# One fused attention and two-layer expert kernel: scores placed behind q, a shorter preparation of the extra unit, and first loads in another order

## The chip, the cores and the metric

The kernel runs on one core of one Trainium2 chip. The metric is the device time of one execution in microseconds (us); lower is better. The core has TensorE (PE, matrix products), VectorE (DVE), ScalarE (ACT) and GpSimd (POOL) for computing, SyncE (SP) for issuing transfers, and 16 DMA engines. Each engine works through its own list of instructions in order and waits on semaphores for the others. PE writes to PSUM, which has eight banks; a bank is written again only when its readers are done.

## The reference

Three parts, one after another, on 8 batches of 576 tokens with 8 heads of 64 (4608 tokens of width 512):

```python
def sm_attn(qq, kk, vv):                      # softmax(scale * qq kk^T) vv
    ...
p_packed = sm_attn(p, k, v)                   # 32 packed rows per head
x = sm_attn(q, p_packed, p_packed)            # 576 rows per head
# first expert layer: 8 experts, D = 512, F = 1024, one expert per token
y[mask] = gate_w[mask, None] * (np.maximum(x[mask] @ w1[e], 0) @ w2[e])
# second layer: only tokens with x @ w_skip > 0, other weights
out[do_compute] = xc + gate_w * (np.maximum(xc @ w1[e], 0) @ w2[e])
```

## The kernel before

The work runs batch by batch, with everything transposed so that features lie on partitions. Per batch the main generator `gen_M` makes two halves of 288 tokens: `stage1` (lines 728, 733, 734) forms h in eight tiles of six matmuls each, `stage2` (line 749) forms y in four tiles of 24. Each fp32 product is made of three products of a high and a low part: `hh` is ACT's rounded copy of h and `hl` DVE's remainder, `W2h`/`W2l` and `Q1h`/`Q1l` are such pairs of weights. A main batch assumes one expert for the whole batch; tokens that do not fit are handled as extra units (`gen_x`) and, in the second layer, by lists (`gen_pick` and others).

The smaller steps are put between the matmuls of `gen_M` by a planner, `Weave`. It has 48 steps per batch: 8 for h and 16 for y in each half. A side generator gets a window such as `(8, 0.5, 1.06)`: 8 steps spread from 50% to 106% of the loop. With `TE` its steps on PE go to the borders of y tiles. These sides matter here:

- `gen_S(b)` (from line 382), two batches ahead: `heads` (line 385) writes the scores s1 of packed rows p against k into four banks, DVE takes their maxima mx (407) and the negated nm (413), ACT the exponentials a1 (417), PE transposes those (434), and pv, pk, PKT follow.
- `gen_pre(b)` (from 627), one batch ahead: reads the expert index e1 into a register (631), loads W1 by it (642), and multiplies it by PKT (`heads` again, called q1), so that Q1 = W1 folded with the packed values; ACT and DVE cut it into Q1h and Q1l (lines 623, 624).
- `gen_T`, `gen_R(b)` (580): second scores and the products L for the gate of the first layer; `x_flags` (970) turns sums csA into flags of extra units.

SP issues nearly all loads in its list's order. For batch 0 the quarters of k go by SP and ACT in turn. PE fills waits in the head with idle products ("keep", line 347).

Of the kernel before, what the change touches and what calls it, by code (L numbers as in the profile page):

```python
# [11 lines left out]
BF16 = mybir.dt.bfloat16  # L12
# [106 lines left out]
def attn_moe_kernel(ctx, tc, q, k, v, p, wg, w11, w12, w21, w22, out):  # L119
# [18 lines left out]
    def ct(name, shape, dt=F32, fill=None, eng=None):  # L138
        t = const.tile(shape, dt, name=name)
        if fill is not None:  # L140
            (eng or nc.vector).memset(t, fill)
        return t
# [5 lines left out]
    iot = ct("iot", [128, 128])  # L148
    pid = ct("pid", [128, 1])
    E8 = ct("E8", [128, E])  # L150
    M5 = ct("M5", [128, 5, 2, NXP])
    once = ct("once", [128, 5, 32])
    tri = ct("tri", [128, 128])
    ones = ct("ones", [128, 128])
# [214 lines left out]
        return [(t[:, 0:n], a[:, 0:n]), (t[:, n:], a[:, n:])]  # L369

    def load_k(b, *eng):
        ins = load(b, "kT", k, [2, 4, HALF], quarters, eng)
        load(b, "pT", p, [128], lambda t, a: [(t, a)], eng[:1])
        return ins

    def load_v(b, *eng):
        return load(b, "v", v, [10, 4, D], halves, eng)
# [249 lines left out]
    def gen_pre(b):  # L627
        d = us[b]
        while "e1" not in st[b]:
            next(A)  # L630
        e1 = nc.sync.value_load(e1i[0:1, b:b + 1], min_val=0, max_val=E - 1)
        d["e1"] = e1
        W1 = []

        def lw(n):
            for z in range(2):
                if n:
                    w = us[b]["y"].rearrange("p t c -> p (t c)")[:, F * z:F * (z + 1)]
                    w = w.rearrange("p (h f) -> p h f", h=2)
                else:  # L640
                    w = wcp.tile([128, 2, 512], F32, tag="W1c", name="W1c")
                nc.sync.dma_start(
                    out=w,
                    in_=w11[dsn(e1, 1), n, z].rearrange("o p h f -> p (o h) f"),
                )
                W1.append(w)

        lw(0)
        if b > 1:
            us[b]["y"] = bulk.tile([128, 4, S], F32, tag="y", name="y1", bufs=2)  # L650
        lw(1)
        yield
        A2 = st[b]["A2"]
        d["A2h"] = [q1p.tile([128, 2, HALF], F32R, tag=f"A2h{i}", name="A2h") for i in range(2)]
        d["A2l"] = [q1p.tile([128, 2, HALF], F32R, tag=f"A2l{i}", name="A2l") for i in range(2)]

        def halve(hf):
            return split(d["A2h"][hf], d["A2l"][hf], A2[:, :, hf * HALF:(hf + 1) * HALF], nc.vector)

        Q1h = q1p.tile([128, 2, F], F32R, name="Q1h")  # L660
        Q1l = q1p.tile([128, 2, F], F32R, name="Q1l")
        d["Q1"] = (Q1h, Q1l)
        PKT = st[b]["PKT"]
        def product(n):
            ps = [mt("q1") for _ in range(2)]
            heads(ps, PKT, lambda hp: W1[2 * n + hp // 2][:, hp % 2, :], start=True, stop=True)
            return ps

        def cut(n, ps, cuts=()):
            sl = slice(512 * n, 512 * n + 512)  # L670
            for x in range(2):
                with ExitStack() as order:
                    for ins in cuts:
                        order.enter_context(tc.issue_after(ins))
                    split(Q1h[:, x, sl], Q1l[:, x, sl], ps[x], nc.vector)
                yield

        cuts = halve(0)
        if b:
            yield  # L680
            halve(1)
            yield TE
            ps = [product(n) for n in range(2)]
            for n in range(2):
                yield from cut(n, ps[n])
        else:
# [34 lines left out]
    def stage1(lh, ll, rh, rl, kt, hh, hl, hf=None):  # L721
        n_, nr = hh.shape[2], rh.shape[2]
        for f in range(8):
            ps = mt("h")
            n = 0
            for t in range(kt):
                for l, r in ((lh, rh), (lh, rl), (ll, rh)):
                    nc.tensor.matmul(  # L728
                        out=ps[:, 0:nr], lhsT=l[:, t, 128 * f:128 * f + 128], rhs=r[:, t, :],
                        start=(n == 0), stop=(n == 3 * kt - 1),  # L730
                    )
                    n += 1
            nc.scalar.activation(out=hh[:, f, :], in_=ps[:, 0:n_], func=ACTF.Relu)  # L733
            nc.vector.scalar_tensor_tensor(  # L734
                out=hl[:, f, :], in0=ps[:, 0:n_], scalar=0.0, in1=hh[:, f, :].bitcast(F32),
                op0=ALU.max, op1=ALU.subtract,
            )
            if nr > n_:
                nc.vector.tensor_scalar(out=hf[:, f, :], in0=ps[:, n_:nr], scalar1=0.0, scalar2=None, op0=ALU.max)
            yield  # L740
# [196 lines left out]

    us[0]["y"], us[1]["y"] = (bulk.tile([128, 4, S], F32, tag="y", name="y1", bufs=2) for _ in range(2))
    k0 = load_k(0, nc.sync, nc.scalar)
    nc.scalar.dma_start(out=wgAB, in_=wg)  # L940
    behind = mybir.DependencyInfo(mybir.DependencyClass.Sync, mybir.DependencyReason.DATA)
    tc.add_manual_dep(load_v(0, nc.sync)[0], k0[0].name, behind)
    with tc.issue_after(k0[2]):
        load_q(0, nc.sync)
        load_k(1)
        load_q(1)
# [18 lines left out]

    def x_flags():
        f0 = mt("f0")
        for z in range(2):
            for s in range(5):
                nc.tensor.matmul(  # L970
                    out=f0[0:NXP, B * z:B * z + B], lhsT=M5[:, s, z, :], rhs=csA[:, s, :], start=(s == 0), stop=(s == 4)
                )
        FL = X["FL"]
        Fv = FL.rearrange("p (b z) -> p b z", z=2)
# [57 lines left out]
                out=EB["W2"][:, :, 128 * t:128 * t + 128], in_=w12[dsn(ex, 1), t].rearrange("o p f c -> p (o f) c")  # L1032
            )

    def gen_x(X):
        li = X["li"]
        A2g, bd, xt, hr, hx, ro, yx = (X[n] for n in ("A2", "bd", "xt", "hq", "hx", "rq", "y"))
        for hp in range(4):
            r = slice(32 * hp, 32 * hp + 32)
            nc.vector.tensor_tensor(  # L1040
                out=bd[r, :, hp, :], in0=A2g[r], in1=X["gB"][r].unsqueeze(1).to_broadcast([32, 2, UW]), op=ALU.mult
            )
        yield
        ps = mt("xt")
        for x in range(2):
# [119 lines left out]

    def gen_pick(d):

        gc, f, cu, po, Og = d["gc"], EB["f"], EB["cu"], EB["po"], EB["O"]
        nc.vector.tensor_scalar(out=f, in0=gc, scalar1=0.0, scalar2=None, op0=ALU.is_gt)
        for j in range(1, 5):  # L1170
            nc.vector.tensor_tensor(out=cu[:, j:j + 1], in0=cu[:, j - 1:j], in1=f[:, j - 1:j], op=ALU.add)
        yield TE
        ps = mt("pk")
        nc.tensor.matmul(out=ps[:, 0:5], lhsT=trib, rhs=f, start=True, stop=False)
        nc.tensor.matmul(out=ps[:, 0:5], lhsT=oneb, rhs=cu[:, 0:5], start=False, stop=True)
        nc.vector.tensor_copy(po, ps[:, 0:5])
        for j in range(5):
            nc.vector.tensor_scalar(
                out=Og[:, j, :], in0=iot, scalar1=po[:, j:j + 1], scalar2=gc[:, j:j + 1],
                op0=ALU.is_equal, op1=ALU.mult,  # L1180
            )
# [178 lines left out]
    for b in range(B):  # L1360
# [4 lines left out]
        if b + 2 <= B:  # L1365
# [8 lines left out]
                sides.append((gate(b, 2), 2, 0.4, 0.48))  # L1374
            if b + 2 < B:
                if b:
                    plan = ((NS, 0.06, 0.18, TE), (NT, 0.18, 0.477), (8, 0.5, 1.06))
                else:
                    plan = ((2, 0.04, 0.075), (5, 0.115, 0.235), (NT, 0.235, 0.48), (8, 0.5, 1.06))
            else:  # L1380
                plan = ((NS, 0.06, 0.17, TE), (NT, 0.17, 0.33), (NR, 0.34, 0.52))
            sides += [(part(A, n), n, *w) for n, *w in plan]
        if b + 1 < B:
            pre = gen_pre(b + 1)
            w2 = gen_w2(w12, us[b + 1], False)
            sides.append((chain(part(pre, 1), part(w2, 1)), 2, 0.5, 0.6))
            sides.append((part(pre, 2), 2, 0.7, 0.85))
            sides.append((pre, 5, 0.88, 1.0, TE))
            if b + 2 == B:
                sides.append((gen_gB(b + 1), 2, 0.97, 1.0))  # L1390
            sides.append((w2, 4, 0.76, 1.1))
        if b < B - 1:
            W = Weave(gen_M(b), NM, sides, EVERY if b else 2)
        if b == B - 2:
            W.run(0.53)
            run_gen(A)
            a_ctx.close()
            ep = e1_ctx.enter_context(tc.tile_pool(name="ep", bufs=1))
# [13 lines left out]
            X["bd"] = X["ro"][:, 256:512].rearrange("p (x h c) -> p x h c", x=2, c=UW)  # L1412
            X["li"] = xs.tile([1, 3], I32, name="xli")
            cx = X["cx"] = xs.tile([32, 3], F32, name="cx")
            EB["cu"] = xs.tile([128, 5], BF16, name="ecu")
            nc.vector.memset(EB["cu"], 0.0)
            nc.vector.memset(X["bd"], 0.0)
            EB["gc"] = [xs.tile([128, 5], F32, name=f"egc{i}") for i in range(2)]
            EB["gB"] = [xs.tile([128, S], F32, name=f"egB{i}") for i in range(2)]
# [26 lines left out]
        elif b == B - 1:  # L1446
# [22 lines left out]
            with c.Else():  # L1469
                first_half(True)  # L1470
            d0.update(e_load(lyA, iA, 0, True, False))
            W = Weave(gen_M(b, (1,)), NM // 2, [])
            W.run(1 / 3)
            q1_ctx.close()
# [31 lines left out]
    EB["hr"] = X["h"]  # L1506
    EB["xT"] = X["ro"].rearrange("p (t c) -> p t c", t=4)
    ds = {}
    cA = nc.values_load(lyA[3:4, 0:1], min_val=0, max_val=1)

    def gen_load(s):
        d = e_load(lyB, slice(s + 1, s + 2), s + 1, True)
# [201 lines left out]
```

## Time and profile before

| | |
|---|---|
| time, median of 3 runs | 596.32 us (596.19 to 596.82) |
| the profiled execution | 596.14 us, of which span 594.4 us |
| PE busy | 578.4 us (97%) |
| DVE, ACT, POOL busy | 337.4, 216.7, 135.3 us |
| mean granted clock of PE | 0.998 |

The span is the time from the first to the last instruction that the profiler saw. Busy time of PE is counted from the start of a matmul to its modelled end, so matmuls that overlap are not counted twice, and a busy PE can still be off its usual pace. In the timeline a row is a run of like instructions: its start, the time it covers, and in brackets how long the engine was idle before it and for whom it waited. The trace counts one fp32 matmul as two records in some shapes, so block s of 16 matmuls is 32 records.

### The profile page before, as it was taken

The numbers are of one execution on the slowest core, as the hardware profiler recorded it, in microseconds if no ns is written. First come the engines' busy times: TensorE is split into PE (matmuls) and PEld (weight loads), VectorE is DVE, ScalarE is ACT, GpSimd is POOL, SyncE is SP. The second block draws the span as 40 slices with busy tenths as digits, with TensorE's granted clock in tenths as the row PEclk, the third lists the DMA queues.
The fourth block names the chain that finished last, engine by engine and source line by source line (L and its number), as shares of the span: only waits on it lengthen the run. The fifth ranks groups of instructions, "written<-read, shape, count | busy, mean of one in ns | idle before, by whom it ended". The sixth has DMA issues, their size and how long they took to land.

```text
span 594.4 us, 14695 instructions
## 1 busy us (share of the span) xinstructions
PE 578.4 (97%) x5901; PEld 532.2 (90%) x5902; DVE 337.4 (57%) x1001; ACT 216.7 (36%) x475; POOL 135.3 (23%) x122
## 2 busy tenths in 40 slices
PE   7799999999999999999999999999999999999996
PEld 5479899989989989989989898899999999999795
DVE  3878468558638738747746864446846336163110
ACT  3463452542553362344345234224414325052110
POOL 4051331241060150141133105020301220140032
PEclk9999999999999999999999999999999999999999
DMA  8987869567647737826715526996147592722064
GB/s 332 354 320 277 343 243 343 173 242 277 246 171 255 281 148 283 305 74 256 271 41 199 206 71 195 323 320 217 48 132 275 72 374 79 204 53 114 1 99 63
DMA packets 35994, 123.05 MB, mean 207 GB/s; under 512 B 5696, under 2 KB 15680, under 8 KB 29888
## 3 DMA queue, kind: packets, MB, share of 16 engines
q1 hardware_dynamic: 30352, 115.80, 53.2%
q0 software_dynamic: 3968, 4.85, 6.2%
q10 hardware_dynamic: 1584, 1.25, 0.7%
q8 instruction: 50, 0.82, 0.6%
q14 instruction: 40, 0.33, 0.2%
HBM read 92.62 MB, written 29.26 MB: 205 GB/s over the span
## 4 chain that ended last, share of the span: by engine, by line
PE 74%; another core or an unknown queue 6%; DVE 5%; DMA 5%; issue 3%; SPq 2%; ACT 1%; POOL 1%; POOLq 0%; DVEq 0%
PE y L749 30%; PE h L728 23%; PE y L1338 9%; PE s L385 3%; PE q L385 2%; DMA out_dram<-iXR 2%; SPq L1031 1%; DMA gm2d<-gT 1%; PE L L793 1%; PE pv L447 1%; PE at L434 1%; DMA pT<-in_p_dram 1%; DMA egB<-gm2d 1%; PE L L580 1%
## 5 line engine op out<-in xcount | busy, mean ns | idle before, releaser
L749 PE MATMUL y<-hh,W2h 128*128 128x288 f32 x512 | 155.4, 303 | 0.5 <-ACT hh L733 0.5
L749 PE MATMUL y<-hl,W2h 128*128 128x288 f32 x512 | 151.3, 296 | 0.8 <-DVE hl L734 0.6
L749 PE MATMUL y<-hh,W2l 128*128 128x288 f32 x512 | 150.8, 294 | 0.0
L749 PEld LDWEIGHTS y<-hh,W2h 128*128 128x128 f32 x512 | 96.0, 187 | 10.7 <-issue 6.6
L749 PEld LDWEIGHTS y<-hl,W2h 128*128 128x128 f32 x512 | 96.2, 188 | 1.4 <-DVE hl L734 1.4
L624 POOL TENSOR_TENSOR W2l<-W2c,W2h 128x1024 fp32r<-128x1024 f32 x28 | 67.0, 2400 | 131.1 <-ACT W2h L623 112.0
L749 PEld LDWEIGHTS y<-hh,W2l 128*128 128x128 f32 x512 | 96.4, 188 | 0.3 <-issue 0.3
L728 PE MATMUL h<-A2h,Q1h 128*128 128x288 f32 x256 | 77.3, 302 | 2.0 <-DVE T L527 2.0
L734 DVE SCALAR_TENSOR_TENSOR hl<-h,hh 128x288 fp32r<-128x288 f32 x128 | 57.2, 452 | 35.1 <-ACT hh L733 34.1
L728 PE MATMUL h<-A2h,Q1l 128*128 128x288 f32 x256 | 75.5, 296 | 0.0
L728 PE MATMUL h<-A2l,Q1h 128*128 128x288 f32 x256 | 75.3, 295 | 0.0
L733 ACT ACTIVATE hh<-h 128x288 fp32r<-128x288 f32 x128 | 52.3, 413 | 61.3 <-PE h L728 57.0
L728 PE MATMUL h<-eXh,eW1h 128*128 128x288 f32 x192 | 57.7, 300 | 0.7 <-DMA x2d<-y 0.7
L1338 PE MATMUL y<-ihh,iW2h 128*128 128x288 f32 x192 | 56.8, 296 | 0.0
L1338 PE MATMUL y<-ihh,iW2l 128*128 128x288 f32 x192 | 56.6, 295 | 0.0
L728 PE MATMUL h<-eXl,eW1h 128*128 128x288 f32 x192 | 56.5, 295 | 0.0
L1338 PE MATMUL y<-ihl,iW2h 128*128 128x288 f32 x192 | 56.5, 294 | 0.0
L728 PE MATMUL h<-eXh,eW1l 128*128 128x288 f32 x192 | 56.5, 294 | 0.0
L728 PEld LDWEIGHTS h<-A2h,Q1h 128*128 128x128 f32 x256 | 48.0, 187 | 6.1 <-ACT Q1h L623 2.9
L728 PEld LDWEIGHTS h<-A2h,Q1l 128*128 128x128 f32 x256 | 48.1, 188 | 0.6 <-DVE Q1l L624 0.5
L623 ACT CAST W2h<-W2c 128x1024 fp32r<-128x1024 f32 x30 | 31.7, 1055 | 45.4 <-DMA W2c<-in_w_dram 18.3
L728 PEld LDWEIGHTS h<-A2l,Q1h 128*128 128x128 f32 x256 | 48.1, 188 | 0.0
(300 smaller groups left out, 949.8 us busy)
## 6 DMA issues: line engine op xcount, KB each, us to landing
eW<-in_w_dram SPq DMA_DIRECT2D x8, 2048.0 KB
W2c<-in_w_dram SPq DMA_DIRECT2D x30, 512.0 KB
y<-in_w_dram SPq DMA_DIRECT2D x18, 512.0 KB
v<-in_v_dram SPq DMA_DIRECT2D x7, 1280.0 KB
W1c<-in_w_dram SPq DMA_DIRECT2D x16, 512.0 KB
kT<-in_k_dram SPq DMA_DIRECT2D x7, 1152.0 KB
qT<-in_q_dram SPq DMA_DIRECT2D x7, 1152.0 KB
x2d<-y SPq DMA_DIRECT2D x7, 1152.0 KB
```

Source lines behind the costliest of these rows:

```text
L385: m = nc.tensor.matmul(out=out[x][32 * hp:32 * hp + 32], lhsT=lhsT[64 * x:64 * x + 64, 32 * hp:32 * hp + 32], rhs=rhs(hp)[64 * x:64 * x + ...
L434: last = nc.tensor.transpose(ats[x][:, 128 * j:128 * j + 128], a1[:, x, 128 * j:128 * j + 128], ident).ins
L447: nc.tensor.matmul(out=pv[x][32 * hp:32 * hp + 32], lhsT=aT[:, 4 * x + j, 32 * hp:32 * hp + 32], rhs=vm[:, 2 * hp + x, j, :], start=(j == ...
L580: nc.tensor.matmul(out=L[32 * i:32 * i + 32, 0:LN], lhsT=gs[:, g, :], rhs=A2[:, g, c:c + LN], start=(g == 0), stop=(g == 1),)
L623: a = nc.scalar.copy(out=hi, in_=x)
L624: z = eng.tensor_tensor(out=lo, in0=x, in1=hi.bitcast(F32), op=ALU.subtract)
L728: nc.tensor.matmul(out=ps[:, 0:nr], lhsT=l[:, t, 128 * f:128 * f + 128], rhs=r[:, t, :], start=(n == 0), stop=(n == 3 * kt - 1),)
L733: nc.scalar.activation(out=hh[:, f, :], in_=ps[:, 0:n_], func=ACTF.Relu)
L734: nc.vector.scalar_tensor_tensor(out=hl[:, f, :], in0=ps[:, 0:n_], scalar=0.0, in1=hh[:, f, :].bitcast(F32), op0=ALU.max, op1=ALU.subtract,)
L749: nc.tensor.matmul(out=ps[:, 0:HALF], lhsT=l[:, f, :], rhs=r[:, f, :], start=(n == 0), stop=(n == 23))
L793: nc.tensor.matmul(out=L[32 * i:32 * i + 32, 0:LN], lhsT=wgB[:, t, :], rhs=y1[:, t, LC[i]:LC[i] + LN], start=(t == 0), stop=(t == 3),)
L1338: nc.tensor.matmul(out=ps[:, 0:HALF], lhsT=l[:, f, 128 * t:128 * t + 128], rhs=r[:, f, c], start=(n == 0), stop=(n == 23))
```

## The change

```diff
-    M5 = ct("M5", [128, 5, 2, NXP])
+    M5 = ct("M5", [128, 5, 2, NXP], BF16)
+    csb = ct("csb", [128, 5, B], BF16)
...
     def load_k(b, *eng):
-        ins = load(b, "kT", k, [2, 4, HALF], quarters, eng)
-        load(b, "pT", p, [128], lambda t, a: [(t, a)], eng[:1])
-        return ins
+        load(b, "pT", p, [128], lambda t, a: [(t, a)], eng[1:])
+        return load(b, "kT", k, [2, 4, HALF], quarters, eng)
...
+        ea = e1 if b else nc.scalar.value_load(e1i[0:1, b:b + 1], min_val=0, max_val=E - 1)
...
-                nc.sync.dma_start(
-                    out=w,
-                    in_=w11[dsn(e1, 1), n, z].rearrange("o p h f -> p (o h) f"),
-                )
+                eng, e = (nc.scalar, ea) if b == 0 and z > n else (nc.sync, e1)
+                eng.dma_start(out=w, in_=w11[dsn(e, 1), n, z].rearrange("o p h f -> p (o h) f"))
...
     k0 = load_k(0, nc.sync, nc.scalar)
-    nc.scalar.dma_start(out=wgAB, in_=wg)
...
-    tc.add_manual_dep(load_v(0, nc.sync)[0], k0[0].name, behind)
-    with tc.issue_after(k0[2]):
+    v0 = load_v(0, nc.sync)
+    tc.add_manual_dep(v0[0], k0[0].name, behind)
+    with tc.issue_after(v0[1]):
+        wg0 = nc.sync.dma_start(out=wgAB, in_=wg).ins
+    with tc.issue_after(wg0):
         load_q(0, nc.sync)
         load_k(1)
         load_q(1)
...
     def x_flags():
         f0 = mt("f0")
+        nc.vector.tensor_scalar(out=csb, in0=csA, scalar1=0.0, scalar2=None, op0=ALU.is_gt)
...
-    ... lhsT=M5[:, s, z, :], rhs=csA[:, s, :], ...
+    ... lhsT=M5[:, s, z, :], rhs=csb[:, s, :], ...
...
-    def gen_x(X):
+    def gen_x(X, tail=None):
+        last = tail["hl"] if tail else None
...
+            with tc.issue_after(last) if last is not None else nullcontext():
                 nc.vector.tensor_tensor(
                     out=bd[r, :, hp, :], in0=A2g[r], in1=X["gB"][r].unsqueeze(1).to_broadcast([32, 2, UW]), op=ALU.mult
                 )
...
-        for j in range(1, 5):
-            nc.vector.tensor_tensor(out=cu[:, j:j + 1], in0=cu[:, j - 1:j], in1=f[:, j - 1:j], op=ALU.add)
...
-        nc.tensor.matmul(out=ps[:, 0:5], lhsT=oneb, rhs=cu[:, 0:5], start=False, stop=True)
+        for j in range(4):
+            nc.tensor.matmul(
+                out=ps[:, j + 1:5], lhsT=oneb, rhs=f[:, j:j + 1].to_broadcast([128, 4 - j]), start=False, stop=(j == 3)
+            )
...
-                    plan = ((NS, 0.06, 0.18, TE), (NT, 0.18, 0.477), (8, 0.5, 1.06))
+                    plan = ((NS, 0.06, 0.18, TE), (NT, 0.18, 0.477), (1, 0.5, 0.57), (7, 0.815, 1.06, TE))
...
-                plan = ((NS, 0.06, 0.17, TE), (NT, 0.17, 0.33), (NR, 0.34, 0.52))
+                plan = ((NS, 0.06, 0.17, TE), (NT, 0.17, 0.33), (4, 0.34, 0.41), (NR, 0.45, 0.56))
...
-            sides.append((pre, 5, 0.88, 1.0, TE))
+            sides.append((pre, 5, 0.8, 1.0, TE))
...
-            W.run(0.53)
+            W.run(0.565)
```

`us[0]["hl"]` is set by `stage1` to its last hl instruction. In the same way batch 0 has its plan's last entry replaced, and `cA`, a register loaded for a branch, is loaded in the source before the last half batch instead of behind it.

The instruction lists show where it moves. On PE in batch 1, at the end of s and of q before (h is L728, y is L749, both scores and q come from line 385):

```order
679 L728 MATMUL h<-A2h,Q1l 128x288
680 L385 MATMUL s_1741<-kT,pT 32x288
...
695 L385 MATMUL s_1752<-kT,pT 32x288
696 L749 MATMUL y<-hh,W2h 128x288
...
767 L749 MATMUL y<-hh,W2l 128x288
768 L385 MATMUL q_1887<-W1c,PKT 32x512
...
783 L385 MATMUL q_1898<-y_1663,PKT 32x512
784 L749 MATMUL y<-hh,W2h 128x288
```

and the same place in the changed kernel:

```order
727 L749 MATMUL y<-hh,W2l 128x288
728 L385 MATMUL q_1822<-W1c,PKT 32x512
...
743 L385 MATMUL q_1833<-y_1673,PKT 32x512
744 L385 MATMUL s_1844<-kT,pT 32x288
...
759 L385 MATMUL s_1855<-kT,pT 32x288
760 L749 MATMUL y<-hh,W2h 128x288
```

Before, 72 y lie between s and q and 24 behind q; after, 48 y lie ahead of q, s follows at once, and 48 y lie behind it.

On PE in batch 6, where L (L580) is formed for batch 7, before:

```order
2402 L749 MATMUL y<-hh,W2l 128x288
2403 L580 MATMUL L<-A_5126,gs 32x160 x2
2404 L749 MATMUL y<-hh,W2h 128x288
2405 L749 MATMUL y<-hl,W2h 128x288
2406 L580 MATMUL L<-A_5126,gs 32x160 x4
2407 L749 MATMUL y<-hh,W2l 128x288
2408 L580 MATMUL L<-A_5126,gs 32x160 x2
2409 L749 MATMUL y<-hh,W2h 128x288
```

and after:

```order
2413 L749 MATMUL y<-hl,W2h 128x288
2414 L749 MATMUL y<-hh,W2l 128x288
2415 L580 MATMUL L<-A_5136,gs 32x160 x8
2416 L749 MATMUL y<-hh,W2h 128x288
2417 L749 MATMUL y<-hl,W2h 128x288
```

The three pieces are one, 12 y further on.

SP's first transfers, before:

```order
3 L358 DMA kT<-in_k_dram 128x576 x2
4 L358 DMA pT<-in_p_dram 128x128
5 L358 DMA v<-in_v_dram 128x1280 x2
6 L358 DMA qT<-in_q_dram 128x1152 x2
7 L358 DMA kT<-in_k_dram 128x2304
8 L358 DMA pT<-in_p_dram 128x128
9 L358 DMA qT<-in_q_dram 128x2304
```

and after:

```order
3 L359 DMA kT<-in_k_dram 128x576 x2
4 L359 DMA v<-in_v_dram 128x1280 x2
5 L944 DMA wgAB<-in_wg_dram 128x256
6 L359 DMA qT<-in_q_dram 128x1152 x2
7 L359 DMA pT<-in_p_dram 128x128
8 L359 DMA kT<-in_k_dram 128x2304
9 L359 DMA qT<-in_q_dram 128x2304
```

The first p has gone to the front of ACT's list, ahead of ACT's two quarters of k, and wgAB has come from ACT's list to behind v; p of batch 1 stands ahead of its k.

## Rows read from the trace of the kernel before

**Rows 1.** The page's chain that ended last: share of the span by engine.

```profile
PE 74%; another core or an unknown queue 6%; DVE 5%; DMA 5%; issue 3%; SPq 2%; ACT 1%; POOL 1%; POOLq 0%; DVEq 0%
```

**Rows 2.** By stretch: length; busy PE, PEld, DVE, ACT, POOL; clock, DMA share, GB/s.

```profile
110.00:157.00 47.00, 47.00 (x551) 43.89 (x543) 30.79 (x96) 19.24 (x46) 12.18 (x6) 1.00 0.67 242
```

**Rows 3.** Timeline, PE around block s: start, length, engine, line, operation, count.

```profile
156.48 0.29 PE L728 MATMUL h<-A2h,Q1l 128*128 128x288 f32 x1
...
158.07 0.30 PE L749 MATMUL y<-hl,W2h 128*128 128x288 f32 x1
```

**Rows 4.** Timeline, PE, a block with its own shape behind it.

```profile
185.05 1.20 PE L385 MATMUL s<-qT,PKT 64*32 64x288 f32 x32
186.04 0.25 PE L385 MATMUL s<-wgAB,PKT 64*32 64x32 f32 x13
```

**Rows 5.** Timeline around q of batch 6, with ACT and DVE.

```profile
361.98 1.09 PE L385 MATMUL q<-W1c,PKT 64*32 64x512 f32 x16
362.00 1.05 ACT L623 CAST W2h<-W2c 128x1024 fp32r<-128x1024 f32 x1 [2.95 <-PE y L749]
...
362.86 1.06 PE L385 MATMUL q<-y,PKT 64*32 64x512 f32 x16
...
363.16 2.06 ACT L623 CAST Q1h<-q 128x512 fp32r<-128x512 f32 x4
363.78 1.89 DVE L624 TENSOR_TENSOR Q1l<-q,Q1h 128x512 fp32r<-128x512 f32 x3 [1.23 <-ACT Q1h L623]
```

**Rows 6.** Timeline, DVE and ACT behind block s.

```profile
158.49 1.54 DVE L407 TENSOR_REDUCE mx<-s 128x1 f32<-128x288 f32 x4
...
160.25 0.50 ACT L417 ACTIVATE a<-s,nm 128x288 f32<-128x288 f32 x1 [2.47 <-DVE nm L413]
```

**Rows 7.** Timeline, PE in batch 6: first and last y around L's pieces.

```profile
337.27 0.29 PE L749 MATMUL y<-hh,W2l 128*128 128x288 f32 x1
...
340.05 0.30 PE L749 MATMUL y<-hl,W2h 128*128 128x288 f32 x1
```

**Rows 8.** Timeline, PE, L as one block in an earlier batch.

```profile
179.30 0.73 PE L580 MATMUL L<-A,gs 128*32 128x160 f32 x16
179.95 0.40 PE L728 MATMUL h<-A2h,Q1h 128*128 128x288 f32 x1
```

**Rows 9.** Timeline, PE, the flags.

```profile
344.30 1.41 PE L970 MATMUL f<-csA,M 128*72 128x8 f32 x20
345.56 0.38 PE L728 MATMUL h<-A2h,Q1h 128*128 128x288 f32 x1
```

**Rows 10.** Timeline, PE, two bf16 matmuls of the selection.

```profile
529.52 0.18 PE L1174 MATMUL pk<-if,trib 128*128 128x5 bf16 x1
...
529.56 0.17 PE L1175 MATMUL pk<-ecu,oneb 128*128 128x5 bf16 x1
```

**Rows 11.** Timeline, DVE and PE in batch 7: bd, and y.

```profile
369.14 3.14 DVE L1040 TENSOR_TENSOR xro<-xA,xgB 32x64 f32<-32x64 f32 x4 [0.59 <-DVE y L767]
...
378.21 0.40 PE L749 MATMUL y<-hl,W2h 128*128 128x288 f32 x1 [0.63 <-DVE hl L734]
```

**Rows 12.** Chain of waits in the head: start, length, what.

```profile
1.94 5.16 DMA pT<-in_p_dram
...
7.24 1.21 PE s L385 x32
...
17.60 1.38 issue
```

**Rows 13.** Table by stretch, the head (columns as in rows 2).

```profile
4.00:6.00 2.00, 2.00 (x8) 1.41 (x6) 0.00 (x0) 0.00 (x0) 0.65 (x1) 1.00 1.05 398
19.00:20.00 1.00, 1.00 (x25) 0.44 (x24) 0.59 (x2) 0.00 (x0) 0.00 (x0) 1.00 0.18 61
26.80:36.07 9.27, 8.62 (x67) 6.90 (x68) 8.48 (x21) 8.82 (x22) 2.56 (x3) 1.00 0.76 312
```

**Rows 14.** DMA issues of the head: one line of the list.

```profile
wgAB<-in_wg_dram ACTq DMA_DIRECT2D x1, 128.0 KB
```

More of the change, by code (lines that the diff above doesn't have):

```diff
@@ L733, in stage1 @@
             nc.scalar.activation(out=hh[:, f, :], in_=ps[:, 0:n_], func=ACTF.Relu)
-            nc.vector.scalar_tensor_tensor(
+            ins = nc.vector.scalar_tensor_tensor(
                 out=hl[:, f, :], in0=ps[:, 0:n_], scalar=0.0, in1=hh[:, f, :].bitcast(F32),
@@ L737, in stage1 @@
             )
+            us[0]["hl"] = ins.ins
             if nr > n_:
@@ L970, in x_flags @@
                 nc.tensor.matmul(
-                    out=f0[0:NXP, B * z:B * z + B], lhsT=M5[:, s, z, :], rhs=csA[:, s, :], start=(s == 0), stop=(s == 4)
+                    out=f0[0:NXP, B * z:B * z + B], lhsT=M5[:, s, z, :], rhs=csb[:, s, :], start=(s == 0), stop=(s == 4)
                 )
@@ L1039, in gen_x @@
             r = slice(32 * hp, 32 * hp + 32)
-            nc.vector.tensor_tensor(
-                out=bd[r, :, hp, :], in0=A2g[r], in1=X["gB"][r].unsqueeze(1).to_broadcast([32, 2, UW]), op=ALU.mult
-            )
+            with tc.issue_after(last) if last is not None else nullcontext():
+                nc.vector.tensor_tensor(
+                    out=bd[r, :, hp, :], in0=A2g[r], in1=X["gB"][r].unsqueeze(1).to_broadcast([32, 2, UW]), op=ALU.mult
+                )
         yield
@@ L1166, in gen_pick @@
     def gen_pick(d):
-        gc, f, cu, po, Og = d["gc"], EB["f"], EB["cu"], EB["po"], EB["O"]
+        gc, f, po, Og = d["gc"], EB["f"], EB["po"], EB["O"]
         nc.vector.tensor_scalar(out=f, in0=gc, scalar1=0.0, scalar2=None, op0=ALU.is_gt)
-        for j in range(1, 5):
-            nc.vector.tensor_tensor(out=cu[:, j:j + 1], in0=cu[:, j - 1:j], in1=f[:, j - 1:j], op=ALU.add)
         yield TE
@@ L1174, in gen_pick @@
         nc.tensor.matmul(out=ps[:, 0:5], lhsT=trib, rhs=f, start=True, stop=False)
-        nc.tensor.matmul(out=ps[:, 0:5], lhsT=oneb, rhs=cu[:, 0:5], start=False, stop=True)
+        for j in range(4):
+            nc.tensor.matmul(
+                out=ps[:, j + 1:5], lhsT=oneb, rhs=f[:, j:j + 1].to_broadcast([128, 4 - j]), start=False, stop=(j == 3)
+            )
         nc.vector.tensor_copy(po, ps[:, 0:5])
@@ L1376, in attn_moe_kernel @@
                 if b:
-                    plan = ((NS, 0.06, 0.18, TE), (NT, 0.18, 0.477), (8, 0.5, 1.06))
+                    plan = ((NS, 0.06, 0.18, TE), (NT, 0.18, 0.477), (1, 0.5, 0.57), (7, 0.815, 1.06, TE))
                 else:
-                    plan = ((2, 0.04, 0.075), (5, 0.115, 0.235), (NT, 0.235, 0.48), (8, 0.5, 1.06))
+                    plan = ((2, 0.04, 0.075), (5, 0.115, 0.235), (NT, 0.235, 0.48), (1, 0.5, 0.57), (7, 0.815, 1.06, TE))
             else:
-                plan = ((NS, 0.06, 0.17, TE), (NT, 0.17, 0.33), (NR, 0.34, 0.52))
+                plan = ((NS, 0.06, 0.17, TE), (NT, 0.17, 0.33), (4, 0.34, 0.41), (NR, 0.45, 0.56))
             sides += [(part(A, n), n, *w) for n, *w in plan]
@@ L1414, in attn_moe_kernel @@
             cx = X["cx"] = xs.tile([32, 3], F32, name="cx")
-            EB["cu"] = xs.tile([128, 5], BF16, name="ecu")
-            nc.vector.memset(EB["cu"], 0.0)
             nc.vector.memset(X["bd"], 0.0)
@@ L1461, in first_half @@
                 if withx:
-                    gx = gen_x(X)
+                    gx = gen_x(X, us[0])
                     sides += [(part(gx, 7), 7, 0.5, 0.8), (gx, 18, 0.8, 1.0)]
@@ L1471, in attn_moe_kernel @@
             d0.update(e_load(lyA, iA, 0, True, False))
+            cA = nc.values_load(lyA[3:4, 0:1], min_val=0, max_val=1)
             W = Weave(gen_M(b, (1,)), NM // 2, [])
@@ L1508, in attn_moe_kernel @@
     ds = {}
-    cA = nc.values_load(lyA[3:4, 0:1], min_val=0, max_val=1)
     def gen_load(s):
```

## The prediction, before the result was known

> **What bounds the kernel now.** I read the chain of waits first, then tables by stretch, then the timeline where TensorE (PE) works but does not advance. The chain that ended last lies on PE for 74% [rows 1]. In the table by stretch, 110 to 157 us, about one batch, shows 47.00 of 47.00 us busy at a granted clock of 1.00 [rows 2]. There no other engine sets the time: an edit counts if it takes time out of PE's own stream, or if it makes PE wait. So I looked for places where PE is busy but off its usual pace, and for the few real stalls: the head, and one at 378 us.
>
> The pace: neighbouring h and y matmuls start 0.133 us apart (three take 0.40). At a border between these 128-row matmuls and a block of smaller shape it is lost. From the last h at 156.48, past block s, to the second y at 158.07 it is 1.59 us [rows 3]; two matmuls at their pace are 0.27, so s costs 1.32. Another block of the same 32 records, with a block of its own shape behind it, takes 185.05 to 186.04 = 0.99 [rows 4]. A lone block thus pays 1.32 - 0.99 = 0.33 at its two borders.
>
> **The change part by part.**
>
> *s joined with q.* In batches 0 to 5, s no longer stands alone between h and y (in batch 0 between h and h) but right behind q. Both have 64x32 tiles, so q and s share one pair of borders and one pair goes: 6 x 0.33 = 2.0 us. Bounds: if the seam between them costs as much as a border, nothing; at most 0.4 each, 2.4. I take 2.0, since the seam of two such blocks in [rows 4] shows no gap.
>
> What comes behind it: count from q's start, t = 0. q takes two halves of 0.88 (361.98 to 362.86 [rows 5]), s 0.99, borders 0.2 before the next y: PE is there at 2.95, and 48 y later (6.4 us) at the transposes of the exponentials, 9.35. On ACT a W2h cast starts with q and takes 1.05, four Q1h follow in 2.06 from 1.18 [rows 5]. DVE's first Q1l starts at 1.80 and three take 1.89 [rows 5], so the first frees its PSUM bank at 2.43: the y at 2.95 has 0.5 to spare. DVE then takes two of four row maxima, the last Q1l (0.63), the other two (1.54 for four [rows 6]) and the short negated maxima: 3.7 + 0.6 + 1.5 = 5.8, with those about 6.1. ACT follows with four exponentials of 0.50 [rows 6], some 2.1 with gaps: 8.2 to 8.5. PE comes at 9.35: about 0.8 to spare. Before, they were done long before the transposes. W1, which q now needs 24 y (3.2 us) earlier, is asked for at about 0.53 of the loop, and q now stands at step 40 of 48: 0.3 of a loop, some 14 us, lies between. I count no wait, and keep the spare 0.8 for a rival.
>
> *Product L of the last batch (L580).* In batch 6 it stands in three pieces between y matmuls. From 337.27 to 340.05 it is 2.78 us [rows 7] for 16 records and five y; less 5 x 0.133 that is 2.11. One block of 16 at 179.30 lets the next h start at 179.95 [rows 8], 0.65; with 0.33 for borders 1.0. Gain 1.1, in which waits for its inputs are included, that 12 more y ahead of it let pass. Bounds 0 (the waits move along) and 1.4. The route from L to the flags starts 1.6 us later, but 36 matmuls now stand between them on PE, against 33 before: no wait.
>
> *Flags in bf16.* Ten fp32 matmuls are 20 records that hold PE from 344.30 to 345.56 [rows 9], 1.26 us. After, they are ten bf16 ones, which start 0.04 apart (529.52, 529.56 [rows 10]); ten with borders come to 0.6. Gain 0.65. Bounds: a gain of 0.15 if each bf16 matmul takes 0.11 with its weights, 0.9 at the bare pace. The new comparison on DVE (csb) is ready before PE is there.
>
> *Product bd behind the last hl.* Its four DVE multiplications last 3.14 us from 369.14: an operand is still being loaded. The hl of batch 7 queue behind them, and PE's y waits 0.63 for hl at 378.21 [rows 11]. Now bd stands behind the eight hl, PE's use of it later still. Gain 0.6, bounds 0 and 0.7.
>
> *Pick.* Three bf16 matmuls more at 0.04: +0.1. Four small DVE additions less come to nothing, since PE has other work meanwhile. The register load cA moved in the source keeps its place on every engine: 0.
>
> *First loads.* The first s starts at 7.24, released by p, which SP issued third at 1.94 and which landed 5.16 us later [rows 12]. Now p is first on ACT's queue, and wgAB no longer shares the first 7 us. s can go by quarters of k: its first half as soon as the warm-up is done, its second when the last quarter lands. It ended at 8.45; I expect 7.6, and maxima, transposes and the expert index of batch 0 0.8 earlier. What is late next: k and p of batch 1, behind the same bytes as before. Their s is held there, and its stop of 1.38 at 17.60 [rows 12], for which no release shows, stays. DVE's chain to the first h hangs on that s, so I leave the first h where it is. The earlier index lets W1, W2 and the next v go earlier, since the DMA engines are at 0.18 in 19 to 20 us [rows 13]; so the later waits of the head shrink: PE idles 0.65 in 26.8 to 36.07 [rows 13], and a little behind. Half of W1 issued by ACT costs ACT about 1 us where it only waits. Together -0.8; bounds +0.5 (the last k of ACT's queue behind SP's v) and -1.8 (the stop shrinks too).
>
> A rule speaks against this part. The Trainium skill, "DMA: Bandwidth & Descriptors", section "Issuing engines are not separate DMA queues", says that transfers of all issuing engines share the same 16 DMA engines, and that spreading them saves only the sequencer's time to start them. By it the head would gain only what the second rival below gives it; the trace agrees in that the DMA share is 1.05 in 4 to 6 us.
>
> **The sum.** -0.8 - 2.0 - 1.1 - 0.65 - 0.6 + 0.1 = -5.05 us. The durations are from an execution of 596.14 us (span 594.4 and 1.7 around it), 0.18 below the median of 596.32; on the median it is 591.3.
>
> **Rivals.**
> 1. *The joins give nothing:* the seam costs what the borders cost, or the first y waits for its bank, since 0.5 to spare is little. For: q and s use other weights and other banks, and no row shows q followed by s. Against: [rows 4]. Then -3.05: 593.3.
> 2. *The head gains little:* the DMA engines are full at 398 GB/s [rows 13], so k and p land earlier only by the 128 KB of wgAB [rows 14] that leave the way, 0.3 us. Against: p stood behind two quarters of k on its queue and landed last. Then 0.5 less: 591.8; with no gain at all 592.1.
> 3. *The exponentials come late (slower):* in the new order they stand behind q's casts and wait for maxima that stand between DVE's Q1l. Place: the transposes, six batches. Price: what that chain exceeds its spare of 0.8, six times. If another W2h cast (1.05) and one more Q1l (0.63) get ahead of them, they are 0.9 past the spare: 5.4 us, 596.7, the gain is gone; that is the point from which it decides, 1.65 us of lateness. With 0.3 more per batch it is 598.5. For: it is the longest chain that the change builds. Against: ACT and DVE have little else there, and order and durations are known.
>
> **How the numbers follow.** Forecast 0.58, first rival 0.17, second 0.17, third 0.05; the rest mixtures. The forecast's own range is 590.0 to 592.4. For 8 in 10 I go from 589.8 (all upper bounds together give 589.1) to 594.2 (joins and head that gain nothing). About 0.2%, 1.2 us, is what a measurement of this kernel tells from no change: faster by more 0.90, within it 0.06, slower 0.04.
>
> **What would show it.** In the profile after: q and s as neighbours, about 2.95 us from q's start to the next y, no idle before that y or the transposes; L580 as one group of 16; the flags within 0.7 us; no y waiting for hl near 374; the first s before 6.8 us and the stop near 17 still there. I am wrong if PE idles at the transposes in each batch, or if the seam costs 0.3.

## The result, and the profile after

The changed kernel takes 590.38 us (median of 4 runs, 589.88 to 591.78) against 596.37 (596.19 to 596.82) of the kernel before beside it: ratio 0.9902 [0.9884, 0.992], by which it is 5.84 us less (5.99 by the medians). 591.3 (589.8 to 594.2) was predicted. The profiled execution after took 590.5 us, with a span of 588.8. The page, span and busy time by engine:

```profile
span 588.8 us, 14696 instructions
PE 575.2 (98%) x5894; PEld 533.0 (91%) x5895; DVE 332.9 (57%) x997; ACT 217.2 (37%) x475; POOL 134.2 (23%) x122
```

PE's busy time fell by 3.2 us (from 578.4), the span by 5.6: a good half is work that became shorter, the rest waits that went. To place the gain I compare the start of the same h or y matmul in both traces; there are 3456 of them, from the 42nd on in the same order.

| matmul number | before | after | difference | what lies since the row above |
|---|---|---|---|---|
| 1 | 26.80 | 26.23 | -0.57 | head, to the first h |
| 97 | 48.42 | 46.77 | -1.65 | rest of the head |
| 337 | 88.15 | 86.88 | -1.27 | batch 0 with its join |
| 1777 | 325.98 | 322.95 | -3.03 | five joins, then batch 6 |
| 1873 | 342.71 | 338.42 | -4.29 | product L (L580) |
| 1921 | 350.80 | 345.60 | -5.20 | flags |
| 2113 | 385.73 | 379.58 | -6.15 | bd |
| 2305 | 417.63 | 411.81 | -5.82 | branch to the last batch |
| 3409 | 582.05 | 576.27 | -5.78 | pick |

The timeline of the changed kernel, around the join of one batch (PE, ACT, DVE):

```profile
114.25 1.09 PE L385 MATMUL q<-W1c,PKT 64*32 64x512 f32 x16
115.14 1.06 PE L385 MATMUL q<-y,PKT 64*32 64x512 f32 x16
...
115.43 2.05 ACT L623 CAST Q1h<-q 128x512 fp32r<-128x512 f32 x4
...
116.00 1.18 PE L385 MATMUL s<-kT,pT 64*32 64x288 f32 x32
...
116.05 1.88 DVE L624 TENSOR_TENSOR Q1l<-q,Q1h 128x512 fp32r<-128x512 f32 x3 [1.23 <-ACT Q1h L623]
117.10 0.41 PE L749 MATMUL y<-hh,W2h 128*128 128x288 f32 x1
...
117.86 0.81 DVE L407 TENSOR_REDUCE mx<-s 128x1 f32<-128x288 f32 x2
...
121.65 0.51 ACT L417 ACTIVATE a<-s,nm 128x288 f32<-128x288 f32 x1
...
123.61 1.03 PE L434 MATMUL at<-ident,a 128*128 128x128 f32 x8
```

q, q and s start 0.89 and 0.86 apart, without a seam. The next y starts 2.85 after q (2.95 forecast) and has no idle time. The last exponential ends at 122.16, 7.9 after q, and the first transposition starts at 9.36: 1.4 to spare, where 0.8 was forecast. PE could come earlier still: of the eight transposes each pair needs one exponential, and the pair of the last one starts at 124.26, 2.1 behind it.

L and the flags, timeline of PE, after:

```profile
336.03 0.75 PE L580 MATMUL L<-A,gs 128*32 128x160 f32 x16
336.71 0.41 PE L749 MATMUL y<-hh,W2h 128*128 128x288 f32 x1
...
341.61 0.48 PE L973 MATMUL f<-csb,M 128*72 128x8 bf16 x10
341.95 0.38 PE L727 MATMUL h<-A2h,Q1h 128*128 128x288 f32 x1
```

L is one group that holds PE for 0.68 ([rows 7] showed it in pieces); the flags hold it for 0.34, not 1.26 [rows 9]. bd, timeline of DVE, after:

```profile
371.07 0.46 DVE L733 SCALAR_TENSOR_TENSOR hl<-h,hh 128x288 fp32r<-128x288 f32 x1 [0.19 <-ACT hh L732]
...
371.45 0.95 DVE L1045 TENSOR_TENSOR xro<-xA,xgB 32x64 f32<-32x64 f32 x4
```

Behind the last hl its operand is there: 0.95 instead of 3.14, and no y waits for hl [rows 11].

All of PE's longer waits, after (engine, matmul, line, what it waited for: us in total, times, longest):

```profile
PE keep L348 <- DVE fl L852: 1.7, 1, 1.7
PE h L727 <- DVE Q1l L624: 1.5, 1, 1.5
PE s L385 <- issue: 0.9, 1, 0.9
PE h L727 <- issue: 0.8, 1, 0.8
PE h L727 <- DMA x2d<-y: 0.8, 1, 0.8
PE q L385 <- DMA W1c<-in_w_dram: 0.7, 1, 0.7
```

Five of the six lie in the head or at the branch; the fourth is new, in batch 0. Timeline of PE, after:

```profile
84.85 0.30 PE L727 MATMUL h<-A2h,Q1h 128*128 128x288 f32 x1 [0.84 <-issue]
```

### The profile page after: what moved, and what is told of

Same layout as the page of the kernel before. It is cut to its first block, busy times and chain, and to the rows that moved or that the text cites. A ratio compares the mean times of both kernels' runs of the same rounds, so it can differ in the third digit from the quotient of the medians.

```text
span 588.8 us, 14696 instructions
## 1 busy us (share of the span) xinstructions
PE 575.2 (98%) x5894; PEld 533.0 (91%) x5895; DVE 332.9 (57%) x997; ACT 217.2 (37%) x475; POOL 134.2 (23%) x122
## 4 chain that ended last, share of the span: by engine, by line
PE 72%; issue 12%; another core or an unknown queue 7%; DVE 4%; DMA 2%; POOL 1%; POOLq 1%; ACT 0%; DVEq 0%
PE y L749 33%; PE h L727 22%; PE y L1344 4%; PE s L385 3%; PE q L385 2%; DMA out_dram<-iXR 2%; PE L L793 1%; PE keep L348 1%; PE at L434 1%; PE pv L447 1%; PE L L580 1%; DVE eW1l L624 1%; POOL iW2l L624 1%; DVE eXl L624 0%
## 5 line engine op out<-in xcount | busy, mean ns | idle before, releaser
L749 PE MATMUL y<-hh,W2h 128*128 128x288 f32 x512 | 154.6, 302 | 0.0
L749 PE MATMUL y<-hl,W2h 128*128 128x288 f32 x512 | 151.0, 295 | 0.0
L749 PE MATMUL y<-hh,W2l 128*128 128x288 f32 x512 | 150.8, 295 | 0.0
L749 PEld LDWEIGHTS y<-hh,W2h 128*128 128x128 f32 x512 | 96.0, 187 | 5.2 <-DVE Q1l L624 2.8
L749 PEld LDWEIGHTS y<-hh,W2l 128*128 128x128 f32 x512 | 96.4, 188 | 0.0
L749 PEld LDWEIGHTS y<-hl,W2h 128*128 128x128 f32 x512 | 96.1, 188 | 0.0
L767 DVE TENSOR_TENSOR y<-y,gB 128x288 f32<-128x288 f32 x48 | 21.5, 449 | 44.1 <-PE y L749 38.9
```

What stands on the lines that cost most here:

```text
L749: nc.tensor.matmul(out=ps[:, 0:HALF], lhsT=l[:, f, :], rhs=r[:, f, :], start=(n == 0), stop=(n == 23))
L767: nc.vector.tensor_tensor(out=y1[:, t, cols], in0=ps[:, 0:HALF], in1=d["gB"][:, cols], op=ALU.mult)
```

## The experiments

Unless said otherwise an edit is shown against the changed kernel; a ratio is to the kernel before, on the same chip. "At the 97th" is the difference to before at the 97th matmul of the table's counting.

**The joins alone** (against the kernel before; the line of batch 0 likewise):

```
-    plan = (..., (8, 0.5, 1.06))
+    plan = (..., (1, 0.5, 0.57), (7, 0.815, 1.06, TE))
-    sides.append((pre, 5, 0.88, 1.0, TE))
+    sides.append((pre, 5, 0.8, 1.0, TE))
```

> Only the joins: the kernel before, with the plans of batches 0 to 5 and the window of q changed, nothing else. Theory (one pair of borders goes per join; the trace after shows 0.355 per join in batches 1 to 5 and 0.62 in batch 0): 6 joins give -2.4 us; -1.4 if the stop of 0.84 near 84 us, which the changed kernel has in batch 0, comes with the join. Rival (the seam costs what the borders cost): 0.

Ratio 0.9975 [0.9957, 0.9992], 1.5 us less. Its profiled execution was the longest of its eleven (597.69): TensorE ran at 0.50 of its clock in two stretches of the head, and the 97th matmul came 2.4 us later than in the kernel before; at the branch 0.85 more was lost. Batches 1 to 5 gain 0.35 each, as in the changed kernel: the seam of q and s costs nothing, and the first rival falls. Batch 0 gains 0.7 by its join and loses more behind it, since it has the new stop too. Its timeline, PE:

```profile
88.56 0.40 PE L728 MATMUL h<-A2h,Q1l 128*128 128x288 f32 x1 [0.65 <-issue]
```

**The first loads alone** (against the kernel before): p first on ACT's queue, wgAB behind v, and

```
+    eng, e = (nc.scalar, ea) if b == 0 and z > n else (nc.sync, e1)
+    eng.dma_start(out=w, in_=w11[...])
```

> Only the first loads: the kernel before, with p first on ACT's queue, wgAB behind v and W1's second part of batch 0 issued by ACT. Theory (the head gains the start of s and the waits behind it): -1.65 us as in the trace after, where the lower clock in 26 to 29 us is already in it; -3 if the clock stays up here. Rival (DMA engines are full, only wgAB's bytes leave the way): -0.3.

Ratio 0.9984 [0.9971, 0.9998], 0.95 us less; the interval, 0.1 to 1.7, holds both the 1.65 of the theory and the 0.3 of the rival. In the trace it is -0.65 at the 97th, of which 0.49 is lost again within batch 0.

**The extra unit alone:** the changed kernel with the old first loads and the old plans (the two diffs above, undone).

> The rest: the changed kernel with the old first loads and the old places of s and q; so L as one block, flags in bf16, bd behind hl, pick, cA. Theory from the trace after: L -1.2, flags -0.8, bd -0.9, pick and the end of batch 7 +0.3: -2.6 us. By the terms forecast -2.25. Rival (these edits only move waits): 0 to -1.

Ratio 0.9946 [0.9926, 0.9966], 3.2 us less. By the trace: L -1.24, flags -0.91, bd -0.89, branch -0.15, pick +0.07. The three parts by themselves make 1.5 + 0.95 + 3.2 = 5.65, together 5.84: within their intervals, of about 1 us either way, they add up.

**More warm-up products,** to hold the clock in the head:

```
-            keep((10, 14)[b], last)
+            keep((10, 16)[b], last)
...
+                if n == 0:
+                    keep(5)
```

> The changed kernel with idle products of PE where it waits before the first h: keep(16) for keep(14) in batch 1, and keep(5) behind the first q of batch 0. Theory (the granted clock falls to 0.50 in 26.2 to 29.4 us behind a stretch in which PE idles 0.65 and 1.52 us, which costs 12 h at 0.24 for 0.133 us, 1.3 us): clock 1.00 there and -1.3 us against the changed kernel, so -7.1 against before. Rival (waits behind, for v and the casts, take it back): 0 against the changed kernel though the clock stays up.

Ratio 0.9992 [0.9975, 1.001]. The clock was 1.00 all through the head, and yet the whole gain of the change was gone. The head was no better for it (+0.48 at the 97th), and most was lost 390 us later, at the branch. Timeline of PE there, first the changed kernel, then this one:

```profile
409.50 1.55 PE L793 MATMUL L<-y,wgAB 128*32 128x160 f32 x16
411.81 0.37 PE L727 MATMUL h<-eXh,eW1h 128*128 128x288 f32 x1 [0.76 <-DMA x2d<-y]
```

```profile
410.65 1.28 PE L796 MATMUL L<-y,wgAB 128*32 128x160 f32 x16
416.09 0.58 PE L730 MATMUL h<-eXh,eW1h 128*128 128x288 f32 x1 [4.16 <-DMA gm2d<-xgT]
```

PE stood for 4.16 us, 3.4 more than in the changed kernel, and in the 3.4 us behind that it ran at 0.57 of its clock; 1.4 more were lost there. The transfer that the row names can't be what h needs: in the changed kernel it is issued only after the same h has started. What took the time is PE's branch instruction. Its row (how often; duration in ns, least, median, most; first and last start), in the changed kernel and then in this one:

```profile
L1537 PEldq COMPARE_BRANCH  x1: 330/330/330, 411.0 to 411.0; - x1
```

```profile
L1540 PEldq COMPARE_BRANCH  x1: 3747/3747/3747, 411.9 to 411.9; - x1
```

Kinds of DMA traffic from 404 to 417 of this kernel (packets, MB, share):

```profile
q8 instruction: 2, 0.03, 1.1%
```

These are two blocks of 16 KB of instructions. One was in transfer from 412.99 to 414.19, while PE stood at the branch, which ended 1.42 later; the other came at 416.92. In the changed kernel one block came, from 412.34, when PE was past the branch. The theory from this: seven products more ahead of the branch move the block edges of PE's list, and the branch's target is no longer loaded.

**The same products, the same number of instructions:** seven warm-up products of batch 0 are taken away.

```
-            keep((10, 14)[b], last)
+            keep((3, 16)[b], last)
...
+                if n == 0:
+                    keep(5)
```

> The kernel of e4_keep with seven idle products less in the first batch (3 for 10), so that PE's list again has as many instructions ahead of the branch in the last batch as the changed kernel's. Theory (in e4_keep PE stood 4.16 us behind that branch because a block of its instructions had to be loaded, and the seven more products had moved the block's edge): that wait is 0.8 again, one instruction block is loaded there instead of two, and the time is 4 to 5 us shorter than e4_keep's. Rival (the idle products in the head do it by their time or by the clock): the wait of 4 us stays.

Ratio 0.9932 [0.991, 0.9954]: 3.6 us better than the one before, though its head is 1.55 slower than that of the kernel before. Timeline of PE at the branch:

```profile
412.41 1.28 PE L796 MATMUL L<-y,wgAB 128*32 128x160 f32 x16
414.26 0.37 PE L730 MATMUL h<-eXh,eW1h 128*128 128x288 f32 x1 [0.57 <-DMA x2d<-y]
```

The long wait is gone with the count (4 to 5 us had been expected): the branch takes 0.33 again, and one block comes, behind it. The other profiles bear the theory out. PE's list has 9,286 to 9,307 recorded instructions (matmuls, weight loads and the sequencer's own) ahead of this branch in twelve of the fourteen profiles, and there it takes 0.33 or 0.34. It has 9,309 with the seven products, and 9,316 with the joins alone, which have no product more: 3.75 and 1.10, and two blocks each. In the joins' profile the branch ends 1.41 after a block has landed. The Trainium skill, "Runtime: NRT & Kernel Launch", section "Instruction fetch mechanics", says that instructions come in blocks of 16 KiB, one after another, and that a taken branch to a block not at hand must wait for its transfer. The trace agrees (a block in transfer while the branch stood); its price here was the 4.16 us.

**The changed kernel again,** on the chip of three of the others:

> The changed kernel itself again, on this chip, as the measure for the three beside it. Both theories: 590 to 591 us, -5.5 to -6 against before; a stretch of clock 0.50 in the head in some executions.

590.56 (589.74 to 591.25), ratio 0.9897 [0.9875, 0.9919]. In the first profile after, TensorE ran at half its clock just behind the first h. Stretch 26.23 to 29.41 of that profile (length; busy PE, PEld, DVE, ACT, POOL; clock, DMA share, GB/s):

```profile
26.23:29.41 3.18, 3.18 (x13) 2.90 (x13) 2.90 (x10) 2.88 (x10) 0.44 (x1) 0.50 1.03 405
```

This execution had 1.00 there (0.50 only behind 585 us, as all profiles at their end), and comes to -1.49 at the 97th and the same span of 588.8. Waits take up what the low clock costs there: PE idles 0.5 us between 32 and 35 of this execution, not at all in the first. The stop of 0.8 at 85 us came again.

**Batch 0 without its join:** `(8, 0.5, 1.06)` in its plan again.

> The changed kernel with batch 0's s back at its old place between h and h; the joins of batches 1 to 5 stay. Theory (the join of batch 0 gains 0.62 but brings the stop of 0.84 near 84 us with it): the stop is gone from the trace, and the time is the same within 0.4 us. Rival (the stop has nothing to do with the join): it stays, and the time is 0.6 longer than the changed kernel's.

591.28 (590.91 to 591.78), ratio 0.991 [0.9889, 0.9932]: 0.7 above the changed kernel on the same chip, where at most 0.4 was expected, but the intervals overlap. The stop near 85 is gone, but so is the join's 0.7, and batch 0 ends no better (0.33 lost from the 97th on, against 0.38 in the changed kernel). The stop comes with the join and with the count of instructions: of the ten profiles with this join nine have it (0.26 to 0.84). The tenth, the one with seven products more, has none and keeps 0.62 of batch 0's gain; with the count restored it is back, 0.52.

The traces also show what it is. PE stops over 0.2 us without a releaser 22 times in the fourteen profiles: 12 times near 18 us (the stop that the forecast left alone), 9 times at 84 to 88, once at 234 with q later. Each time a 16 KB block of instructions landed 1.21 to 1.55 us before PE went on (in the changed kernel at 83.45, and PE went on at 84.85). And each stop stands behind the same place of PE's list: 449 recorded instructions, 1,985 or 1,986, or 5,314, which is 6 and 19 times 256, or one more, further on. In all, 50 such blocks come for PE's 11,912 recorded instructions, some 240 to a block. So PE had come to the end of a block there, and the next was late. Why it is late at these edges and not at others is not shown.

**q later, 24 y ahead of the transposes:**

```
-    plan = (..., (7, 0.815, 1.06, TE))
+    plan = (..., (7, 0.9, 1.06, TE))
-    sides.append((pre, 5, 0.8, 1.0, TE))
+    sides.append((pre, 5, 0.88, 1.0, TE))
```

> The changed kernel with q and s joined one y tile later (q back at 0.88, s at 0.9), so 24 y instead of 48 stand between them and the transposes. It puts the forecast's third rival to the test. Theory (the chain q, Q1h, Q1l, maxima, exponentials takes 7.9 to 8.1 us from q's start, as in the trace after; PE is at the transposes after 2.85 + 3.2 = 6.05): PE idles 1.9 us at the transposes in each of batches 0 to 5, 11 us in all: 601 to 602. If the maxima can go earlier there, less. Rival (other work fills the gap, or the chain shrinks when PE waits): within 2 us of the changed kernel.

604.4 (603.59 to 605.53), ratio 1.0131 [1.0101, 1.0162]: slower, and by more than the 601 to 602 expected. In the trace each of five batches is 1.9 to 2.1 longer than in the changed kernel, and batch 3, where PE also stops for 1.0 at an edge of its list, 3.8. Timeline (PE, ACT) of one batch, then PE's waits:

```profile
119.56 1.09 PE L385 MATMUL q<-W1c,PKT 64*32 64x512 f32 x16
...
126.61 1.89 PE L434 MATMUL at<-ident,a 128*128 128x128 f32 x8 [0.60 <-ACT a L417]
127.41 0.51 ACT L417 ACTIVATE a<-s,nm 128x288 f32<-128x288 f32 x1
```

```profile
PE at L434 <- ACT a L417: 4.0, 6, 1.0
...
PE y L749 <- DVE Q1l L624: 1.3, 3, 0.7
```

The last exponential ends 8.4 us after q (7.9 in the changed kernel), but PE is there 6.45 after q (126.61 less the 0.60 of idle time) and waits: 4.0 us over the six batches by the list, for the first exponential. Then each pair of transposes goes at the pace of the exponentials; the eight start over 1.6 us instead of 0.8, which is 5 more. Waits of y for Q1l (1.3) and the stop (1.0) bring it to 11 of the 13.7; the rest is not placed. This is the third rival's mechanism at its place: 24 y earlier or later decide between -0.35 and +1.5 or more per batch against the kernel before.

**wgAB back on ACT's queue, behind k:**

```
+    nc.scalar.dma_start(out=wgAB, in_=wg)
-        wg0 = nc.sync.dma_start(out=wgAB, in_=wg).ins
```

> The changed kernel with wgAB on ACT's queue again, behind p and ACT's two quarters of k. Theory (the last quarter of k, on ACT's queue, ends the first s, and wgAB behind it takes nothing from it; v on SP's queue does): s ends as in the changed kernel, 8.1 to 8.4 us, and the time is the same within 0.4 us. Rival (wgAB's 128 KB beside k and v are what the head gains by): s ends 0.3 later, 591.

591.17 (591.02 to 591.64), ratio 0.99 [0.9862, 0.9937]; -0.81 at the 97th. No difference in time that the interval could tell. The last quarter of k landed at 8.53 and the first s ended at 9.26, not at 8.1 to 8.4; two profiles with wgAB behind v and the same length of warm-up (5.49; they follow below) show 8.68 and 9.56, so the rival's 0.3 can't be told.

**p third on SP again:** `load_k` loads p of batch 0 behind k, on SP.

> The changed kernel with p of batch 0 third on SP's queue again, behind SP's two quarters of k; wgAB stays behind v. Theory (p's place only decides which piece lands last; bytes ahead of the last piece are the same): s starts later, near 7, as one block without a gap, and ends at 8.1 to 8.4 as in the changed kernel; 590 to 591. Rival (p first is what the head gains by): s ends 0.8 later and the time is 0.8 longer.

591.67 (590.25 to 592.66), ratio 0.9897 [0.9858, 0.9937]: no loss that shows by time, though its profile, with half the clock from 25 to 32 us, is 1.48 late at the 97th. Timeline of PE, first this kernel, then the changed one:

```profile
6.61 1.21 PE L389 MATMUL s<-kT,pT 64*32 64x288 f32 x32 [0.44 <-DMA pT<-in_p_dram]
7.74 2.58 PE L348 MATMUL keep<-hh 128*128 128x512 f32 x10
```

```profile
6.50 1.69 PE L385 MATMUL s<-kT,pT 64*32 64x288 f32 x32
8.11 2.60 PE L348 MATMUL keep<-hh 128*128 128x512 f32 x10
```

With p behind k the first s ended no later: the product behind it starts at 7.74, against 8.11.

**All of W1 issued by SP:**

```
-    eng, e = (nc.scalar, ea) if b == 0 and z > n else (nc.sync, e1)
+    nc.sync.dma_start(out=w, in_=w11[...])
```

> The changed kernel with all of W1 issued by SP again; the other loads in the new order. Theory (W1's second half an issue of 0.4 to 0.9 us later; W1, W2 and v of batch 1 all land that much later, and the products pv and the casts wait for them in 30 to 42 us): the head's gain of 1.5 us at the end of batch 0's first half falls to about 0.8. Rival (those waits went by the order on ACT and DVE alone): unchanged.

591.65 (591.58 to 592.7), ratio 0.991 [0.988, 0.994]; +1.06 at the 97th. With the same length of warm-up (5.49) the version with wgAB on ACT has -0.81: 1.9 us between them, 0.3 of it because k landed later (8.83 against 8.53). By time the gap is some 0.5, which the intervals don't separate. What the trace shows is an order that flips. ACT around the store of pk, this kernel and then the changed one:

```profile
41.05 0.35 ACTq L461 DMA_DIRECT2D pkd<-pk  x1
41.45 0.41 ACT L730 ACTIVATE hh<-h 128x288 fp32r<-128x288 f32 x1 [2.54 <-PE ps L465]
```

```profile
38.16 0.41 ACT L732 ACTIVATE hh<-h 128x288 fp32r<-128x288 f32 x1 [0.61 <-PE h L727]
39.29 0.35 ACTq L461 DMA_DIRECT2D pkd<-pk  x1
```

And PE's waits from 26 to 50 us of this kernel:

```profile
PE h L725 <- DVE T L527: 1.4, 1, 1.4
PE pv L447 <- ACT hh L730: 0.7, 1, 0.7
PE y L747 <- ACT hh L730: 0.5, 1, 0.5
```

With all of W1 on SP the scheduler puts that hh behind the store, as in the kernel before; PE then waits for hh twice, 0.7 and 0.5. The changed kernel has neither wait. The second lies around the product ps, which needs pk: from the last y ahead of ps to the third behind it the kernel before takes 1.88, the changed one 0.51, and that is its whole gain between the 49th and the 97th (1.38). The order of hh does not decide alone. With wgAB on ACT, hh stands behind the store too, but DVE has pk ready 0.3 behind the first y (1.7 before, 1.6 here), and nearly the same 1.34 is gained; in the kernel with the count restored hh stands ahead, pk comes 2.7 behind the first y, PE waits 1.05 for it and nothing is gained. On SP the same flip: with half of W1 gone from its list, p and k of batch 2 move ahead of the store a2d, which waits for A, and are issued at 23.85 and 24.86 instead of 37.06 and 37.53.

**bd ahead of hl again:** `gx = gen_x(X)`.

> The changed kernel with bd's four multiplications ahead of the hl again. Theory (bd held DVE for 2.4 us and the hl of batch 7 behind it): bd takes some 3 us again, the y near 372 waits, and the time is 0.6 to 0.9 longer than the changed kernel's. Rival (its operand lands earlier by now, since the other edits moved the loads): no wait, same time.

591.89 (591.24 to 592.71), ratio 0.9913 [0.9884, 0.9943]; 0.7 over the version with wgAB on ACT, on the same chip, with intervals that overlap. Timeline, DVE and PE:

```profile
364.32 3.14 DVE L1045 TENSOR_TENSOR xro<-xA,xgB 32x64 f32<-32x64 f32 x4 [0.59 <-DVE y L767]
...
373.39 0.40 PE L749 MATMUL y<-hl,W2h 128*128 128x288 f32 x1 [0.63 <-DVE hl L733]
```

The wait is back as it was, and the trace gains nothing over this stretch where the changed kernel gains 0.89.

## Why the prediction was right, step by step

The total was right, -5.05 forecast and -5.84 measured, within the forecast's own range, and so was the mechanism of joins, L, flags and bd. That of the head was not. Terms of the trace against those of the sum:

- **Joins, -2.0:** 5 x 0.355 = -1.77 in batches 1 to 5, and in batch 0 -0.7 that the new stop (0.84) and what follows it took back. The price of a pair of borders, 0.33, was right, and so was the order of the chain behind it. Its spare was larger than the 0.8: the forecast let the transposes wait for the last exponential, but each pair waits for its own. That batch 0 would lose its share was not foreseen.
- **L, -1.1:** -1.25.
- **Flags, -0.65:** -0.91. The step "ten with borders come to 0.6" was too high: the ten took 0.34, 0.034 each, and the gain is the upper bound that was given.
- **bd, -0.6:** -0.89; undone, all of it lost in the trace. The forecast took the idle time of 0.63 alone. PE's next matmul after a wait takes 0.40 where its neighbours take 0.29, and the two starts lie further apart: the 0.26 beyond the idle time come with the wait.
- **Pick, +0.1:** +0.05. The register load at 0: the branch shows +0.31 here and -0.15 in five of the experiments. Block L793 took 1.55 here and 1.28 there, since its weight loads twice waited for DVE's y (0.30 and 0.22), and the register load stands behind them.
- **Head, -0.8:** -1.65 and -1.49 at the 97th in two profiles, -0.95 by time with the head alone. The sign was right, the path was not. "It ended at 8.45; I expect 7.6" failed: the first s ended at 8.18, in the second profile at 8.40, released by the last quarter of k on ACT's queue, which now stands behind p. Chain of waits in that profile (start, length, what):

```profile
1.89 5.78 DMA kT<-in_k_dram
7.67 0.04 issue
7.71 0.69 PE s L385 x8
```

As for the first loads, the second rival was right: p alone moves nothing. The stop at 17.60, which the forecast left at 1.38, is no part of the gain either: it is 0.94 here, but 0.88 with the old first loads (the extra unit alone) and 1.01 to 1.36 in four other profiles with the new ones. The gain lies at ps, between the 49th and the 97th matmul. Half of W1 on ACT, booked as "costs ACT about 1 us where it only waits", came with another order of hh, pk and the loads of batch 2, which took away the waits that the prediction had only counted as idle time "in 26.8 to 36.07, and a little behind". Which of these reorderings brings pk earlier was not separated.

So the total came nearer than its terms, and that is in part luck: against the sum, L, flags, bd, head and the five joins are off by -0.15, -0.26, -0.29, -0.85 and -0.12, batch 0 and the branch by +0.71 and +0.31. The third rival had its mechanism right, but the changed kernel has 1.4 to spare, by pairs 2.1, and stays clear of it.

Of the Trainium skill's rule in "DMA: Bandwidth & Descriptors", section "Issuing engines are not separate DMA queues", the trace bears out the part on transfers: with p on SP the first s ended at 7.82 to 8.49 in four profiles, with p on ACT at 8.02 to 9.56 in ten. The rest of the head's gain is no counterexample, since it came by the order of instructions.

## What to carry to other kernels

Where one engine is busy all the time, price an edit by the places where it leaves its pace: borders between tile shapes, fp32 matmuls that could be bf16, and waits with the slow matmul behind them. Before a producer is moved nearer to its consumer, add up the whole chain between them; here a spare of some 2 us was what separated -0.35 from +1.5 us per batch. Where a scheduler sets the order, an edit that only takes DMA issues from one engine can reorder the others, so compare the whole lists; and where a branch lies ahead, the number of instructions before it counts too.

## What the runs showed of the hardware that was not expected

- Seven matmuls more, 390 us ahead of a branch, made PE wait 4.16 us at it instead of 0.57, with 1.4 more lost at 0.57 of the clock behind the wait. The branch instruction itself took 3.75 instead of 0.33.
- PE also stopped in straight code, 0.26 to 1.45 us and 22 times in fourteen profiles, at places of its list that lie a multiple of 256 instructions apart (to one); it went on 1.21 to 1.55 behind the landing of a 16 KB block.
- The warm-up's twelve products took from 4.42 to 5.49 us in executions of equal code up to there, which moves the whole head by up to a microsecond; single profiles of the head are to be read with that in mind.
- Some executions showed TensorE at half its clock in the head, the first profile of the changed kernel for 3.2 us behind a wait of 1.5; the same code at 1.00 throughout had the same span.
